# A group's products by the probabilities' high half first, and eight pieces from scores to products

## The chip, the cores and the metric

One core of a Trainium2 chip runs the whole program. The metric is the device time of one execution in microseconds (us). Five engines work beside each other, each through its own list of instructions in order: TensorE (PE, matrix products into PSUM; PEld are its weight loads), VectorE (DVE), ScalarE (ACT), GpSimd (POOL) and SyncE (SP), which here issues most of the DMA transfers.

## The reference

Three layers follow each other on float32 data, 4 sequences of 576 rows, 8 heads of 64:

```python
scores = scale * np.matmul(q, k.transpose(0, 1, 3, 2))      # 4 x 8 x 576 x 576
scores = np.where(block_i >= block_j, scores, -1e9)         # blocks of 64 rows
attn = exp(scores - max) / (sum + 1e-09)
x = np.matmul(attn, v)                                      # then to 2304 x 512
xn = x / rms * rms_g
y = (silu(xn @ w_gate) * (xn @ w_val)) @ w_out              # 512 -> 1536 -> 512
expert_idx = np.argmax(softmax of normed y @ normed experts)
out = gate_w * (relu(y @ w1[e]) @ w2[e])                    # 8 experts, 512 -> 1024 -> 512
```

## The kernel before, in words

Every float32 operand is split into two float16 halves, a high one and the low remainder, and a product is made of three: high by high, high by low, low by high.

**Attention.** Each sequence is cut into tiles of 128 query rows (the fifth has 64), and a tile into groups of heads: 8 heads in one group for the first tile of a sequence, groups of 4 for the second, of 2 for the others; 60 groups in all. A group goes through these steps. `att_qk` (L308) makes the scores on TensorE. `att_max` (L344, VectorE) and `att_exp` (L361, ScalarE) make the probabilities pf. `att_split` (L386) makes the high half ph on ScalarE (L414) and the low half pl on GpSimd (L417; for a sequence's last tile on VectorE, L412) and has SyncE's queue transpose each by DMA into pth and ptl (L423), of which there are two buffers each. `att_pv` (L433) multiplies them with the values: per head and block of 128 keys three products, all adding up in one PSUM tile av: pth with the values' high half, pth with their low half, ptl with their high half (L450 to L452). After a tile's last group `fin_all` (L514) normalizes the result over VectorE, ScalarE and GpSimd and transposes it by DMA into xT (L512), the input of the gate layer. The tile hl that xT is transposed from has one buffer. The first 11 groups are transposed on TensorE instead (L395).

**Gate layer.** Rows are taken in 9 units of 256. For each unit and each of six column steps, `gate_mm` (L519) makes g and v, `gate_t`, `gate_a`, `gate_b` turn them into hT, and `out_mm` (L560) adds hT by w_out into two accumulators o, one for each 128 rows; there are two buffers of o in PSUM. `out_ev` (L572) empties them at a unit's end: a copy, the low half, and a square in place (L579) that is the last to read o. The copy for the second 128 rows also waits for the one buffer R, which a DMA transpose into x2T (L583) has to have read.

**Order.** The groups up to the third unit are put in place by a scheduler that orders each engine's list by simulated times. From there on TensorE's list is written out by hand (L1018 to L1054): the gate layer of six units is a row of 216 pieces, two of out_mm and four of gate_mm for each column step, 12 products of 256 columns or 6 of 512 each. The scores of a group go in at every 4.8 pieces (EVERY) and its products LATER = 7 pieces after its scores:

```python
a = min(pieces - 1, int((g - first) * EVERY) + 2)
due.setdefault(a, []).append(("qk", g))
due.setdefault(min(pieces, a + LATER), []).insert(0, ("pv", g))
```

The other engines' lists are still ordered by the scheduler. **Experts.** After the last unit the tokens are sorted by expert, gathered, and multiplied with the experts' weights (from about 620 us on); that order is written by hand for all engines.

Of the kernel before, what the change touches and what calls it, by code (L numbers as in the profile page):

```python
# [18 lines left out]
P = 128  # L19
# [12 lines left out]
def attention_moe_moe(ctx: ExitStack, tc: tile.TileContext, q, k, v, w_gate, w_val, w_out, rms_g, emb, tau, w1, w2, out):  # L32
    nc = tc.nc
    B, H, S, D = q.shape
# [50 lines left out]
    st_p = p1.enter_context(tc.tile_pool(name="st", bufs=3))  # L85

    FS, PET = 5, 4
    AHEAD, NW0, NW1, NW2, WLAG, NLAG, LOADS, PREPS, PRI, EVERY, LATER = 3, 4, 2, 2, 2, 1, 3, 1, 300, 4.8, 7


    idn = const.tile([P, P], F32, name="idn")
# [131 lines left out]
    nat, qT, kT, vT = {}, {}, {}, {}  # L223

    def rows_of(t):
        return min(P, S - t * P)
# [203 lines left out]
    NOSYNC = mybir.DependencyInfo(mybir.DependencyClass.NoSync, mybir.DependencyReason.DATA)  # L430
    gv = {}

    def att_pv(b, t, heads):  # L433
        pth, ptl = pt_t.pop((b, t, heads[0]))
        if (b, t) not in av:
            av[b, t] = [ps_a.tile([P, H, D], F32, tag="av", name="av"), None]
        a = av[b, t]
        n = rows_of(t)
        nkb = t + 1
        last = t == NTT - 1  # L440
        for j, h in enumerate(heads):
            o = a[0][0:n, h, :]
            for kb in range(nkb):
                kn = min(P, S - kb * P)
                if last:
                    lh, ll = pth[0:kn, kb, 64 * j:64 * j + 64], ptl[0:kn, kb, 64 * j:64 * j + 64]
                else:
                    lh, ll = pth[:, j * nkb + kb, :], ptl[:, j * nkb + kb, :]
                vv = vT[b, kb]
                for i, (x, w) in enumerate(((lh, vv[0:kn, h, 0:D]), (lh, vv[0:kn, h, D:2 * D]), (ll, vv[0:kn, h, 0:D]))):  # L450
                    first = a[1] is None
                    mm = nc.tensor.matmul(out=o, lhsT=x, rhs=w, start=first, stop=(h == H - 1 and kb == nkb - 1 and i == 2), skip_group_check=True)  # L452
                    if first:
                        a[1] = mm.ins
                    else:
                        tc.add_manual_dep(mm.ins, a[1].name, NOSYNC, reason="the first of a bank starts it")
        if heads[-1] == H - 1:
            fin_all(b, t)

# [54 lines left out]
    def fin_all(b, t):  # L514
        for z in (fin_a, fin_b, fin_c, fin_d1, fin_d2, fin_d3):
            z(b, t)
# [358 lines left out]
    for u in range(NU):  # L875
        b, t = max((i, bt) for i, bt in enumerate(TILES) if spot[bt][0] == u)[1]
# [67 lines left out]
    def attend():  # L944
        attend_a()
        att_pv(*groups[state["g"] - 1])
# [71 lines left out]
    first = state["g"]  # L1018
    pieces = NFP * 6 * (NU - 3)
    due = {}  # L1020
    for g in range(first, len(groups)):
        a = min(pieces - 1, int((g - first) * EVERY) + 2)
# [23 lines left out]
    with tc.manual_schedule(engines={ENG.PE}):  # L1046
        for i in range(pieces + 1):
            for kind, g in due.get(i, []):
                if kind == "qk":
                    attend_a(LOADS + 1, PREPS + 1)  # L1050
                else:
                    att_pv(*groups[g])
            if i < pieces:
                piece(2 + i // (6 * NFP), i // 6 % NFP, i % 6)  # L1054
# [149 lines left out]
```

## Time and profile before

| | |
|---|---|
| median of 3 runs | 874.27 us (872.91 to 879.01) |
| the profiled execution | 875.68 us, its span 873.8 us |
| TensorE busy | 791.7 us, 91% |
| VectorE, ScalarE, GpSimd busy | 457.0, 449.6, 354.2 us |
| mean granted TensorE clock | 0.967 |

A timeline row gives the start in us from the span's start, the duration in us, the engine, the line of the kernel, the operation, its output and inputs, shapes and how many like it are merged (x12); in brackets how long the engine had been idle before it and whose end it waited for. SPq is SyncE's queue: the time of its rows is the issue of a transfer, not its flight. The granted clock is 1.00 at 2.4 GHz and 0.50 at 1.2 GHz.

### The profile page before, as it was taken

The page shows a single profiled execution, that of the slowest core. Times are in us where ns is not written, and L with a number is a line of the kernel's source. Part 1 is how long each engine was busy: PE and PEld are TensorE (multiplying, and loading weights), DVE is VectorE, ACT ScalarE, POOL GpSimd, SP SyncE. Part 2 cuts the span into 40 slices and gives each one's busy share as a digit, 9 for nine tenths or more (in the row PEclk, how much of TensorE's full clock was granted, in tenths as well). Part 3 has the DMA queues.
Part 4 walks back from the last instruction along what each step waited for, and adds up shares of the span by engine and source line. Part 5 has one row for each costly group of instructions (what it writes and reads, how often), then busy time and mean ns, then how long its engine had stood idle before and what let it go on. Part 6 is the DMA issues. An engine that isn't in the chain of part 4 may idle for free. (4 is left out here: it accounts for less than half of the span.)

```text
span 873.8 us, 21877 instructions
## 1 busy us (share of the span) xinstructions
PE 791.7 (91%) x8566; PEld 599.1 (69%) x8566; DVE 457.0 (52%) x971; ACT 449.6 (51%) x929; POOL 354.2 (41%) x360
## 2 busy tenths in 40 slices
PE   2769799889899899899899999998989998999994
PEld 2669577668677677677677777757567776667771
DVE  6899978634356445356445453225451265462352
ACT  6988776856556655556555441223311364452352
POOL 5555466756444737434737322212322121302110
PEclk9889889989999999999999999999999999999998
DMA  8574799885777775767875341214546399797694
GB/s 240 158 193 140 180 235 225 151 161 104 134 154 137 122 145 104 148 134 132 136 135 100 65 92 23 49 43 105 169 123 210 83 281 315 187 334 199 158 261 131
DMA packets 297629, 135.37 MB, mean 155 GB/s; under 512 B 250844, under 2 KB 281735, under 8 KB 297514
## 3 DMA queue, kind: packets, MB, share of 16 engines
q1 hardware_dynamic: 289706, 117.26, 61.7%
q0 software_dynamic: 4016, 10.56, 4.0%
q10 hardware_dynamic: 3792, 6.03, 2.1%
q8 instruction: 70, 1.15, 0.6%
q14 instruction: 45, 0.37, 0.1%
HBM read 129.30 MB, written 10.25 MB: 160 GB/s over the span
## 5 line engine op out<-in xcount | busy, mean ns | idle before, releaser
L529 PE MATMUL g<-xT,wg 128*128 128x256 f16 x1296 | 159.2, 278 | 4.2 <-DVE t L546 3.1
L529 PE MATMUL v<-xT,wv 128*128 128x256 f16 x1296 | 156.2, 274 | 0.0
L566 PE MATMUL o<-wo,hT 128*128 128x512 f16 x648 | 153.0, 385 | 3.4 <-ACT o L579 3.1
L529 PEld LDWEIGHTS <-wg 128*128 128x128 f16 x1296 | 126.8, 100 | 28.4 <-issue 4.6
L529 PEld LDWEIGHTS <-wv 128*128 128x128 f16 x1296 | 123.7, 98 | 15.2
L753 PE MATMUL h<-xt,whi 128*128 128x128 f16 x1280 | 109.8, 219 | 1.7 <-DMA xt<-xg 1.7
L753 PE MATMUL h<-xt,wlo 128*128 128x128 f16 x640 | 108.5, 219 | 0.2 <-DVE wlo L720 0.2
L566 PEld LDWEIGHTS <-hT 128*128 128x128 f16 x648 | 61.3, 98 | 68.2 <-issue 5.6
L720 DVE SCALAR_TENSOR_TENSOR wlo<-raw,whi 128x1024 f16<-128x1024 f32 x64 | 76.6, 1222 | 59.5 <-ACT whi L719 53.8
L753 PEld LDWEIGHTS <-whi 128*128 128x128 f16 x1280 | 98.9, 98 | 6.5 <-issue 2.6
L777 PE MATMUL o<-whi,hl 128*128 128x512 f16 x320 | 97.5, 387 | 5.2 <-ACT whi L719 2.8
L554 POOL TENSOR_TENSOR hT<-h,hT 128x512 f16<-128x512 f32 x54 | 64.2, 1189 | 77.3 <-ACT hT L553 75.3
L719 ACT ACTIVATE whi<-raw 128x1024 f16<-128x1024 f32 x64 | 65.9, 1053 | 52.5 <-DMA raw<-in_moe_w_dram 39.5
L417 POOL TENSOR_TENSOR pl<-pf,ph 128x512 f16<-128x512 f32 x66 | 69.5, 1074 | 50.4 <-issue 43.4
L777 PEld LDWEIGHTS <-hl 128*128 128x128 f16 x480 | 46.8, 99 | 62.6 <-issue 12.8
L785 POOL DMA_INDIRECT out_dram<-ob,ido x18 | 20.1, 1116 | 158.9 <-ACTq L726 76.4
L353 DVE TENSOR_REDUCE nb<-sc 128x1 f32<-128x384 f32 (+3 forms) x88 | 54.0, 635 | 45.7 <-PE sc L321 45.5
L452 PE MATMUL av<-vT,ptl 128*128 128x64 f16 (+2 forms) x480 | 56.7, 197 | 23.2 <-DMA ptl<-pl 15.9
L452 PE MATMUL av<-vT,pth 128*128 128x64 f16 (+2 forms) x960 | 64.8, 197 | 10.3 <-DMA pth<-ph 7.4
L452 PEld LDWEIGHTS <-pth 128*128 128x128 f16 (+2 forms) x960 | 52.9, 104 | 20.8 <-DMA pth<-ph 9.3
L372 ACT ACTIVATE pf<-sc,nb 128x128 f32<-128x128 f32 (+3 forms) x128 | 65.9, 526 | 2.3 <-PE v L529 0.4
L452 PEld LDWEIGHTS <-ptl 128*128 128x128 f16 (+2 forms) x480 | 45.3, 104 | 28.1 <-DMA ptl<-pl 18.3
(215 smaller groups left out, 1284.7 us busy)
## 6 DMA issues: line engine op xcount, KB each, us to landing
raw<-in_moe_w_dram SPq DMA_DIRECT2D x172, 512.0 KB
st<-in_moe_w_out_dram SPq DMA_DIRECT2D x12, 512.0 KB
st<-in_moe_w_gate_dram SPq DMA_DIRECT2D x11, 512.0 KB
st<-in_moe_w_val_dram SPq DMA_DIRECT2D x11, 512.0 KB
x2s<-R ACTq DMA_DIRECT2D x18, 256.0 KB
nat<-in_k_dram SPq DMA_DIRECT2D x16, 256.0 KB
nat<-in_q_dram SPq DMA_DIRECT2D x16, 256.0 KB
nat<-in_v_dram SPq DMA_DIRECT2D x16, 256.0 KB
```

Source lines behind the costliest of these rows:

```text
L353: nc.vector.tensor_reduce(out=nb[:, z], in_=sc[:, 0:hpb * keys].rearrange("p (j k) -> p j k", k=keys), axis=AX.X, op=ALU.max)
L372: nc.scalar.activation(out=pf[:, j * keys:(j + 1) * keys], in_=scs[j // hpb][:, (j % hpb) * keys:(j % hpb + 1) * keys], func=ACTF.Exp, sca ...
L417: nc.gpsimd.tensor_tensor(out=pl[:, z:y], in0=pf[:, z:y], in1=ph[:, z:y], op=ALU.subtract)
L452: mm = nc.tensor.matmul(out=o, lhsT=x, rhs=w, start=first, stop=(h == H - 1 and kb == nkb - 1 and i == 2), skip_group_check=True)
L529: mm = nc.tensor.matmul(out=o[:, j, :], lhsT=w[cw][:, kt, f * P:(f + 1) * P], rhs=x[:, cx * KD + kt, :], start=(n == 0), stop=(n == 3 * KD ...
L554: nc.gpsimd.tensor_tensor(out=hT[1][fp], in0=h, in1=hT[0][fp], op=ALU.subtract)
L566: mm = nc.tensor.matmul(out=o, lhsT=hT[ch][f // 2][:, f % 2, j * P:(j + 1) * P], rhs=wo[cw][:, f, :], start=(f == 0 and n == 0), stop=(f = ...
L719: nc.scalar.activation(out=whi[l][c], in_=raw[l][c], func=ACTF.Copy, scale=ES)
L720: nc.vector.scalar_tensor_tensor(out=wlo[l][c], in0=raw[l][c], scalar=ES, in1=whi[l][c], op0=ALU.mult, op1=ALU.subtract)
L753: mm = nc.tensor.matmul(out=h[:, f, :], lhsT=w[:, kt, :], rhs=x[:, cx * KD + kt, :], start=(n == 0), stop=(n == 3 * KD - 1))
L777: nc.tensor.matmul(out=o, lhsT=x[:, cx, kt, :], rhs=w, start=(n == 0), stop=(n == 3 * K2 - 1))
L785: nc.gpsimd.indirect_dma_start(out=out, out_offset=bass.IndirectOffsetOnAxis(ap=(ido if ids is None else ids)[:, i:i + 1], axis=0), in_=ob ...
```

## The change

In `att_pv` the three products of a head and key block no longer stand together: a loop over the two halves is put around the heads, so that all products with pth of a group come first, two for each head and key block, and then all with ptl. LATER is 8 instead of 7.

```diff
--- before.py
+++ after.py
@@ -85,7 +85,7 @@
     st_p = p1.enter_context(tc.tile_pool(name="st", bufs=3))
 
     FS, PET = 5, 4
-    AHEAD, NW0, NW1, NW2, WLAG, NLAG, LOADS, PREPS, PRI, EVERY, LATER = 3, 4, 2, 2, 2, 1, 3, 1, 300, 4.8, 7
+    AHEAD, NW0, NW1, NW2, WLAG, NLAG, LOADS, PREPS, PRI, EVERY, LATER = 3, 4, 2, 2, 2, 1, 3, 1, 300, 4.8, 8
 
 
     idn = const.tile([P, P], F32, name="idn")
@@ -438,22 +438,22 @@
         n = rows_of(t)
         nkb = t + 1
         last = t == NTT - 1
-        for j, h in enumerate(heads):
-            o = a[0][0:n, h, :]
-            for kb in range(nkb):
-                kn = min(P, S - kb * P)
-                if last:
-                    lh, ll = pth[0:kn, kb, 64 * j:64 * j + 64], ptl[0:kn, kb, 64 * j:64 * j + 64]
-                else:
-                    lh, ll = pth[:, j * nkb + kb, :], ptl[:, j * nkb + kb, :]
-                vv = vT[b, kb]
-                for i, (x, w) in enumerate(((lh, vv[0:kn, h, 0:D]), (lh, vv[0:kn, h, D:2 * D]), (ll, vv[0:kn, h, 0:D]))):
-                    first = a[1] is None
-                    mm = nc.tensor.matmul(out=o, lhsT=x, rhs=w, start=first, stop=(h == H - 1 and kb == nkb - 1 and i == 2), skip_group_check=True)
-                    if first:
-                        a[1] = mm.ins
-                    else:
-                        tc.add_manual_dep(mm.ins, a[1].name, NOSYNC, reason="the first of a bank starts it")
+
+        for side in range(2):
+            for j, h in enumerate(heads):
+                o = a[0][0:n, h, :]
+                for kb in range(nkb):
+                    kn = min(P, S - kb * P)
+                    x = (pth, ptl)[side]
+                    x = x[0:kn, kb, 64 * j:64 * j + 64] if last else x[:, j * nkb + kb, :]
+                    vv = vT[b, kb]
+                    for w in (vv[0:kn, h, 0:D], vv[0:kn, h, D:2 * D])[:2 - side]:
+                        first = a[1] is None
+                        mm = nc.tensor.matmul(out=o, lhsT=x, rhs=w, start=first, stop=(side == 1 and h == H - 1 and kb == nkb - 1), skip_group_check=True)
+                        if first:
+                            a[1] = mm.ins
+                        else:
+                            tc.add_manual_dep(mm.ins, a[1].name, NOSYNC, reason="the first of a bank starts it")
         if heads[-1] == H - 1:
             fin_all(b, t)
 
```

TensorE's list at the first group whose stall stands among the rows below at 221.97 us, where its products begin (wv_192 and wo_193 are weight tiles, hT_3_204 the gate layer's result). Before:

```order
L529 MATMUL v<-xT,wv_192 128x256
L452 LDWEIGHTS pth
L452 MATMUL av<-vT,pth 128x64
L452 LDWEIGHTS pth
L452 MATMUL av<-vT,pth 128x64
L452 LDWEIGHTS ptl
L452 MATMUL av<-vT,ptl 128x64
```

And with the change:

```order
L566 MATMUL o<-wo_193,hT_3_204 128x512
L452 LDWEIGHTS pth
L452 MATMUL av<-vT,pth 128x64
L452 LDWEIGHTS pth
L452 MATMUL av<-vT,pth 128x64
L452 LDWEIGHTS pth
L452 MATMUL av<-vT,pth 128x64
```

The group now stands behind a piece of the output product that followed it before, and 16 products with pth stand ahead of the first of the 8 with ptl.

SyncE's queue where the second sequence ends and the third begins, the issues from 278 to 300 us (a shape is that of the transpose; nat are loads for a later tile). Before:

```order
L423 DMA_TRANSPOSE pth<-ph 128x8x128
L423 DMA_TRANSPOSE ptl<-pl 128x8x128
L512 DMA_TRANSPOSE xT<-hl 128x8x64
L423 DMA_TRANSPOSE pth<-ph 128x8x128
L423 DMA_TRANSPOSE ptl<-pl 128x8x128
L232 DMA nat<-in_k_dram 128x8x64
L232 DMA nat<-in_q_dram 128x8x64
L232 DMA nat<-in_v_dram 128x8x64
L423 DMA_TRANSPOSE pth<-ph 128x8x128
L423 DMA_TRANSPOSE ptl<-pl 128x8x128
L512 DMA_TRANSPOSE xT<-hl 128x8x128
```

And with the change:

```order
L423 DMA_TRANSPOSE pth<-ph 128x8x128
L423 DMA_TRANSPOSE ptl<-pl 128x8x128
L423 DMA_TRANSPOSE pth<-ph 128x8x128
L512 DMA_TRANSPOSE xT<-hl 128x8x64
L423 DMA_TRANSPOSE ptl<-pl 128x8x128
L232 DMA nat<-in_k_dram 128x8x64
L232 DMA nat<-in_q_dram 128x8x64
L232 DMA nat<-in_v_dram 128x8x64
L423 DMA_TRANSPOSE pth<-ph 128x8x128
L512 DMA_TRANSPOSE xT<-hl 128x8x128
L423 DMA_TRANSPOSE ptl<-pl 128x8x128
```

Both transposes of xT now stand between a group's pth and its ptl. The third sequence's end has the same two moves.

SyncE's queue ahead of a sequence's fourth and fifth tile, the issues from 233 to 243 us (pth of 128x5x128 belongs to the fifth tile). Before:

```order
L423 DMA_TRANSPOSE pth<-ph 128x8x128
L290 DMA_TRANSPOSE qT<-qd 128x8x128 x2
L423 DMA_TRANSPOSE ptl<-pl 128x8x128
L232 DMA nat<-in_k_dram 128x8x64
L232 DMA nat<-in_q_dram 128x8x64
L232 DMA nat<-in_v_dram 128x8x64
L423 DMA_TRANSPOSE pth<-ph 128x5x128
```

And with the change:

```order
L423 DMA_TRANSPOSE pth<-ph 128x8x128
L290 DMA_TRANSPOSE qT<-qd 128x8x128
L423 DMA_TRANSPOSE ptl<-pl 128x8x128
L232 DMA nat<-in_k_dram 128x8x64
L232 DMA nat<-in_q_dram 128x8x64
L232 DMA nat<-in_v_dram 128x8x64
L290 DMA_TRANSPOSE qT<-qd 128x8x128
L423 DMA_TRANSPOSE pth<-ph 128x5x128
```

One of the two transposes of qT has gone behind ptl and the loads. The same move stands once more, one sequence later.

## Rows read from the trace of the kernel before

**Rows 1.** the page, busy time of TensorE over the span (us, share, instructions)

```profile
PE 791.7 (91%) x8566; PEld 599.1 (69%) x8566; DVE 457.0 (52%) x971; ACT 449.6 (51%) x929; POOL 354.2 (41%) x360
```

**Rows 2.** stretches: us, busy of PE, PEld, DVE, ACT, POOL; granted clock, DMA share, GB/s

```profile
100.00:150.00 50.00, 44.58 (x458) 34.53 (x456) 41.11 (x81) 35.52 (x81) 29.10 (x27) 0.90 1.10 226
200.00:250.00 50.00, 46.73 (x546) 35.99 (x544) 22.56 (x61) 28.30 (x63) 30.39 (x29) 1.00 0.66 119
```

**Rows 3.** waits of TensorE, 150 to 560 us: total, times, longest (us)

```profile
PE av L452 <- DMA ptl<-pl: 15.9, 15, 2.2
PE av L452 <- DMA pth<-ph: 3.0, 2, 2.7
```

**Rows 4.** timeline of TensorE: start, us, instruction, idle before it and who ended it

```profile
173.73 0.20 PE L452 MATMUL av<-vT,ptl 128*128 128x64 f16 x1 [1.61 <-DMA ptl<-pl]
186.80 0.20 PE L452 MATMUL av<-vT,ptl 128*128 128x64 f16 x1 [0.74 <-DMA ptl<-pl]
221.97 0.20 PE L452 MATMUL av<-vT,ptl 128*128 128x64 f16 x1 [0.58 <-DMA ptl<-pl]
241.16 0.20 PE L452 MATMUL av<-vT,ptl 128*128 128x64 f16 x1 [2.21 <-DMA ptl<-pl]
294.36 0.20 PE L452 MATMUL av<-vT,ptl 128*128 128x64 f16 x1 [1.76 <-DMA ptl<-pl]
301.80 0.20 PE L452 MATMUL av<-vT,ptl 128*128 128x64 f16 x1 [0.61 <-DMA ptl<-pl]
369.52 0.20 PE L452 MATMUL av<-vT,ptl 128*128 128x64 f16 x1 [1.98 <-DMA ptl<-pl]
424.32 0.20 PE L452 MATMUL av<-vT,ptl 128*128 128x64 f16 x1 [1.73 <-DMA ptl<-pl]
432.17 0.20 PE L452 MATMUL av<-vT,ptl 128*128 128x64 f16 x1 [1.02 <-DMA ptl<-pl]
449.27 0.20 PE L452 MATMUL av<-vT,ptl 128*128 128x64 f16 x1 [0.95 <-DMA ptl<-pl]
473.28 0.20 PE L452 MATMUL av<-vT,ptl 128*128 128x64 f16 x1 [0.83 <-DMA ptl<-pl]
```

**Rows 5.** timeline of TensorE: two pieces of the output product, then the next piece

```profile
222.62 2.75 PE L566 MATMUL o<-wo,hT 128*128 128x512 f16 x12
225.21 1.47 PE L529 MATMUL g<-xT,wg 128*128 128x256 f16 x12
```

**Rows 6.** timeline of the SyncE queue: start and issue time of transposes

```profile
233.51 1.23 SPq L423 DMA_TRANSPOSE pth<-ph  x1
234.84 2.67 SPq L290 DMA_TRANSPOSE qT<-qd  x2
298.52 1.23 SPq L423 DMA_TRANSPOSE ptl<-pl  x1
299.85 1.29 SPq L512 DMA_TRANSPOSE xT<-hl  x1
```

**Rows 7.** timeline of GpSimd at the same place

```profile
298.45 1.16 POOL L510 TENSOR_TENSOR hl<-x,hl 128x512 f16<-128x512 f32 x1
```

**Rows 8.** stretches after two longer waits, columns as in rows 2

```profile
190.00:195.00 5.00, 4.47 (x25) 2.69 (x25) 0.91 (x3) 0.48 (x2) 2.40 (x4) 0.50 1.00 220
369.50:375.00 5.50, 5.48 (x68) 4.42 (x70) 1.85 (x5) 2.30 (x4) 2.84 (x3) 0.69 1.03 191
```

**Rows 9.** timelines of TensorE and ScalarE: output product, and the square that frees its buffer

```profile
190.53 2.72 PE L566 MATMUL o<-wo,hT 128*128 128x512 f16 x6 [3.09 <-ACT o L579]
320.18 2.75 PE L566 MATMUL o<-wo,hT 128*128 128x512 f16 x12
321.06 0.19 ACT L579 ACTIVATION_READ_ACCUMULATOR o<-o 128x1 f32 x1
451.06 2.75 PE L566 MATMUL o<-wo,hT 128*128 128x512 f16 x12
451.76 0.19 ACT L579 ACTIVATION_READ_ACCUMULATOR o<-o 128x1 f32 x1
```

## The prediction

> **What bounds the kernel now.** I read the page first: TensorE is busy for 91% of the span [rows 1], so the end is set by its work and by the gaps in it. Then the stretches of 50 us. In the attention-and-gate part, from 200 us on, TensorE is busy 46.7 of 50 us at the full clock while VectorE, ScalarE and GpSimd do 22 to 31 [rows 2]: TensorE alone is the limit, and only its waits can be saved. In the stretch from 100 to 150 us it is different: VectorE is busy 41 of 50 us and the DMA engines are loaded above their count (share 1.10) [rows 2], so an order of TensorE's products is not what sets that part's length. Third, the list of waits: from 150 to 560 us TensorE sits idle 15.9 us for the transposed low half ptl, in 15 waits, and 3.0 us for the high half pth, in 2 [rows 3]. Each of the 15 sits at the same place in the timeline: a group's first two products, with pth, start, the third needs ptl, and since the products run in order, everything behind it stands too, the other 14 pth products and the gate products alike [rows 4].
>
> **The change, part by part.**
>
> *The number of instructions* does not change: the same products and weight loads, in another order. It costs nothing by itself.
>
> *High half first.* After a wait the other 22 products of a group of 24 and the next instruction follow within 222.62 - 221.97 = 0.65 us [rows 4, 5], 0.03 us each. Fourteen more pth products now stand ahead of the first ptl product: 14 x 0.03 = 0.41 us more time for ptl to land. It hides work of 0.41 us under the flight and no more; it cannot remove a wait of 2 us.
>
> *One piece more.* Two pieces of the output product take 225.21 - 222.62 = 2.59 us [rows 5], so a piece is 1.30 us of TensorE work, and each group's products now come that much later after its scores. Together ptl gets 1.71 us.
>
> *What that removes.* I count the waits of the manually ordered part. The first two of the 15, 1.61 and 0.74 us [rows 4], lie in the overlap of the scheduled part with it, and I leave them as they are. That leaves 15.9 - 2.35 = 13.55 us in 13 waits. Taken singly only 2.21, 1.76, 1.98 and 1.73 us [rows 4] exceed 1.71. But two things come on top. First, a group's lead contains the products of the group before it. Where that group's stall goes, the lead shrinks by it. This holds for the waits at 301.80 us (0.61, after 1.76) and 432.17 us (1.02, after 1.73) [rows 4]. Second, the queue order moves, as the order of the change shows. At those same two places, where a batch ends, the transpose of xT now stands between pth and ptl, and on GpSimd hl stands ahead of pl. In the trace xT came after ptl and its issue took 1.29 us [rows 6], hl took 1.16 us [rows 7]; I charge 1.2 us, since the two lie beside each other; the bounds are 0, if hl is long ready, and 2.45, if they add up. Residues: 0.61 + 1.76 - 1.71 + 1.2 = 1.86 us, and 1.02 + 1.73 - 1.71 + 1.2 = 2.24 us, with 0.05 and 0.02 us at 294.36 and 424.32 us. At 241.16 and 369.52 us, the longest waits, the order helps: ptl stood behind two transposes of qT, 2.67 us to issue [rows 6], and now stands behind one, so it gains 1.3 us beside the 1.71 and nothing is left. Sum: 13.55 - 4.17 = 9.4 us gained, between 6.9 and 11.8 by the bounds of the xT price.
>
> *The clock.* After the wait of 1.98 us the granted clock of the next 5.5 us was 0.69 [rows 8]: 5.5 x 0.31 = 1.7 us lost to products at the lower level, 1.2 GHz. No other of the 13 waits lies in a stretch that shows this (200 to 250 us holds 2.21 us and has 1.00 [rows 2]). With that wait gone I take 1.7 us; the bounds are 0 and 1.7.
>
> *What is late next.* The output accumulators. At a unit's start the second output piece overwrites a buffer that ScalarE's square must have left. At 320.18 us that piece starts 1.30 us later, at 321.48, and the square ended at 321.06 + 0.19 = 321.25; at 451.06 us it is 452.36 against 451.95 [rows 9]. The slack is 0.23 and 0.41 us. TensorE arrives there earlier by the stall taken out just ahead, 0.95 us at the second place [rows 4], so 0.95 - 0.41 = 0.5 us comes back there and, with a stall of about half a microsecond, 0.3 at the first: 0.8 us, between 0 and 1.2.
>
> *The xT of a finished tile* starts one piece, 1.30 us, later. The tile's unit begins 9 pieces or more after its last products, more than 11 us, and I charge nothing; if that cover were gone, each of the six units would lose up to 1.30 us.
>
> *The scheduled parts*, up to about 190 us, get the high-half-first order too and, through it, another order on every engine. What this is worth the trace does not show. TensorE's sum there is the same, VectorE and the DMA queues carry that part [rows 2], and I take 0. The bounds are 3.0 us either way, the size of the waits for pth there [rows 3]: they may vanish or come once more.
>
> Sum: 9.4 + 1.7 - 0.8 = 10.3 us. The profiled execution took 875.68 us, so 865.4; it lies 1.41 us above the median of the runs, and against that median, 874.27, the forecast is **864 us**.
>
> *A rule against it.* The third transposed group's pth was issued at 233.51 us [rows 6], while the group two before it, which held the same of two buffers, had finished its products when the output product began at 222.62 us [rows 5]: 10.9 us to spare, of which the change uses 1.30. The Trainium skill (Perfetto Trace Analysis, Identifying Performance Opportunities) reads a repeating gap on the saturated engine as a possible lack of buffers for the next tile. By that rule a greater distance would only hold the buffers longer, the transposes would start a piece later, and the result would be that of the first rival below. The trace does not agree with it here: the 10.9 us speak against it.
>
> **The rivals.**
>
> *The piece is given back* (chance 0.20). The pth and ptl of a later group start later by as much as the products moved, because the two buffers of each, or the queue in front of them, free later. Then only the 0.41 us of the first part remain: of the nine listed waits in that part 7.98 us are left, of the other four, 1.88 us in all, some 0.2; the gain is 13.55 - 8.2 = 5.3 us, no clock comes back, 0.8 goes to the accumulators: 4.5 us, **869.8 us**. For it speaks that SyncE's queue is in order and that xT, which itself waits for the moved products, now stands ahead of ptl at batch ends; against it the 10.9 us.
>
> *The scheduled part gains too* (0.19). The 1.61 and 0.74 us [rows 4] and the 3.0 us for pth [rows 3] go with the rest: 864 - 5.35 = **858.6 us**. For it: those are waits for the same tiles. Against it: they lie where DMA is full.
>
> *Slower: the accumulators become the bound* (0.07). At the first unit's start TensorE waited 3.09 us for the square [rows 9], and the next 5 us ran at clock 0.50 [rows 8], another 2.5 us. If the products that used to stand between the two output pieces now stand behind both, and the other five unit starts all wait like this, they cost 5 x 5.59 = 28 us against the 10.3 gained: 17.7 us slower, **892 us**. It decides from the point where the square ends later than the second output piece, a slack of 0.23 and 0.41 us at two of the starts [rows 9]; to be over 1% slower, four of five starts must lose the full price. Against it: the transpose x2T that holds the square up stands no later in the queue now.
>
> *No gain* (0.02): the scheduled part loses what the manual part gains, 874 us.
>
> **How the numbers follow.** The forecast has 0.52, with a range of its own of 860 to 868 (3.0 us of the scheduled part, and the bounds of the xT price). The bound of what a measurement can tell is 1%, or 865.5 us; some six tenths of the forecast's range lie below it. Faster by over 1%: 0.32 + 0.19 = 0.51. Within 1%: 0.20 + 0.20 + 0.02 = 0.42. Slower: 0.07. The range of 855 to 872 us takes in the forecast, the first two rivals and their spread, and leaves out the accumulators.
>
> **What would show it.** Right: the wait for ptl from 150 to 560 us falls from 15.9 to about 6 us, most of it at the two batch ends and in the overlap; no wait at the places of 241.16 and 369.52 us, and the clock there at 1.00; TensorE's busy time the same but for that clock; a wait for the square of under 1 us at the unit starts. Wrong: ptl waits of the same number, each shorter by about 0.4 us (the piece given back); waits for the output accumulators or for xT of a microsecond or more at most unit starts; or a first 190 us longer or shorter by more than 3 us, which would say that the scheduler's new order outweighs what was changed on purpose.

## The result, and the profile after

The change is slower: 882.62 us (876.4 to 886.45, 20 runs) against 877.37 us (871.74 to 883.28, 20 runs) of the kernel before; the ratio is 1.0059, 95% interval 1.0035 to 1.0082. That is 5.2 us more where 10.3 us less was forecast, outside the range of 855 to 872 us and inside the 1% that counted as no change. (3.1 us of the distance from 864 to 882.62 are the kernel before itself, 877.37 us in 20 runs for 874.27 in the three of the forecast.) The profiled execution has a span of 880.9 us and a mean clock of 0.962.

The page's busy line of the kernel after answers to [rows 1]; below it stands that of kernel 12, the kernel before profiled once more as a control. A stretch answers to [rows 2]:

```profile
PE 802.4 (91%) x8566; PEld 606.8 (69%) x8566; DVE 457.3 (52%) x971; ACT 448.5 (51%) x929; POOL 354.1 (40%) x360
```

```profile
PE 798.0 (91%) x8566; PEld 602.4 (69%) x8566; DVE 458.4 (52%) x971; ACT 449.7 (51%) x929; POOL 355.3 (41%) x360
```

```profile
200.00:250.00 50.00, 48.07 (x547) 37.63 (x545) 23.69 (x60) 27.43 (x59) 27.14 (x26) 0.97 0.62 117
```

In that stretch TensorE is busy 48.07 us for 46.73, at a granted clock of 0.97 for 1.00. The same 8566 instructions keep TensorE busy 10.7 us longer than in the profile of before. An edit that only takes waits out leaves the busy time as it is, so this is a hint that part of the loss is inside TensorE's work. It is no proof: in the control the kernel before is itself 6.3 us above its other profile. The waits of TensorE from 150 to 560 us, answering to [rows 3]:

```profile
PE av L452 <- DMA ptl<-pl: 11.0, 8, 1.9
PE av L452 <- DMA pth<-ph: 4.8, 4, 2.3
PE o L566 <- ACT o L579: 1.9, 3, 0.7
```

The waits for ptl are fewer (8 for 15), but two waits for pth have joined them, and the one wait for an accumulator, 3.09 us [rows 9], has become three of 1.9 us in all. TensorE's timeline, the waits of the hand-ordered part that answer to [rows 4] and [rows 9]:

```profile
196.39 0.59 PE L566 MATMUL o<-wo,hT 128*128 128x512 f16 x1 [0.46 <-ACT o L579]
229.13 0.26 PE L452 MATMUL av<-vT,ptl 128*128 128x64 f16 x3 [1.93 <-DMA ptl<-pl]
263.50 0.22 PE L452 MATMUL av<-vT,pth 128*64 128x64 f16 x1 [0.87 <-DMA pth<-ph]
309.22 0.26 PE L452 MATMUL av<-vT,ptl 128*128 128x64 f16 x3 [1.45 <-DMA ptl<-pl]
327.27 0.38 PE L566 MATMUL o<-wo,hT 128*128 128x512 f16 x1 [0.73 <-ACT o L579]
358.82 0.26 PE L452 MATMUL av<-vT,ptl 128*128 128x64 f16 x3 [1.56 <-DMA ptl<-pl]
391.83 0.25 PE L452 MATMUL av<-vT,pth 128*64 128x64 f16 x2 [1.20 <-DMA pth<-ph]
439.03 0.26 PE L452 MATMUL av<-vT,ptl 128*128 128x64 f16 x3 [1.36 <-DMA ptl<-pl]
457.03 0.38 PE L566 MATMUL o<-wo,hT 128*128 128x512 f16 x1 [0.69 <-ACT o L579]
```

From 200 us on that is 9.8 us (ptl 6.3, pth 2.1, accumulators 1.4) for 13.5 before. The waits at the former 241.16 and 369.52 us are gone, as forecast; those at 309.22 and 439.03 us are the two ends of a sequence; the other four, at 229.13, 263.50, 358.82 and 391.83 us, were not forecast. The first of these is not wholly new: the same group waited 0.58 us before [rows 4] and 1.58 us in the control.

One source of longer work is seen in the groups of a sequence's last tile. They have 30 products, as each of the two heads has four key blocks of 128 rows and a fifth of 64. TensorE's timeline of one of them before, then the same group after:

```profile
379.18 0.25 PE L452 MATMUL av<-vT,pth 128*64 128x64 f16 x2
...
379.55 0.20 PE L452 MATMUL av<-vT,ptl 128*64 128x64 f16 x1
379.68 0.25 PE L452 MATMUL av<-vT,pth 64*64 64x64 f16 x2
379.76 0.19 PE L452 MATMUL av<-vT,ptl 64*64 64x64 f16 x1
379.88 0.25 PE L452 MATMUL av<-vT,pth 128*64 128x64 f16 x2
...
380.59 0.28 PE L529 MATMUL g<-xT,wg 128*128 128x256 f16 x1
```

```profile
382.62 1.16 PE L452 MATMUL av<-vT,pth 128*64 128x64 f16 x20
383.71 0.84 PE L452 MATMUL av<-vT,ptl 128*64 128x64 f16 x10
384.48 0.72 PE L529 MATMUL v<-xT,wv 128*128 128x256 f16 x5
```

Read the starts, not the durations. Inside a shape products follow each other by 0.03 us; the first of a 64-row block starts 0.13 us behind its neighbour (379.55 to 379.68), and so does the first of 128 rows behind it (379.76 to 379.88). Each step between the two shapes costs about 0.1 us. Before, a group takes such a step four times, in and out of the fifth block of each head, and lasts 380.59 - 379.18 = 1.41 us. With the halves apart every head meets its fifth block twice: eight steps and 384.48 - 382.62 = 1.86 us. (1.86 - 1.41) / 4 = 0.11 us a step; I take 0.115 from the mean of the groups. There are 16 such groups: 16 x 0.46 = 7.4 us, an estimate that takes the four groups of the scheduled part, where other instructions stand between the products, to cost the same.

Last, where in the program the time is lost. ScalarE's square of the first unit's second rows and of the last but one unit, before and after, and the first of the two in kernel 17, whose lists up to there are those of before:

```profile
189.79 0.58 ACT L579 ACTIVATE o<-o 128x512 f32<-128x512 f32 x1 [0.24 <-DVE R L578]
...
587.50 0.58 ACT L579 ACTIVATE o<-o 128x512 f32<-128x512 f32 x1 [0.76 <-DVE R L578]
```

```profile
195.65 0.58 ACT L579 ACTIVATE o<-o 128x512 f32<-128x512 f32 x1 [0.76 <-DVE R L578]
...
593.22 0.58 ACT L579 ACTIVATE o<-o 128x512 f32<-128x512 f32 x1 [0.76 <-DVE R L578]
```

```profile
196.18 0.58 ACT L579 ACTIVATE o<-o 128x512 f32<-128x512 f32 x1 [0.24 <-DVE R L578]
```

In this pair 5.9 us are gone by the end of the scheduled part, and the hand-ordered part takes 397.6 us after for 397.7 before (399.6 in the control). But kernel 17 comes to that square later still, with the lists of before. A pair of profiles therefore does not place the loss; kernels 5 and 9 below, each of one part alone, do.

### The profile page after: what moved, and what is told of

It reads as the page before. It is cut to its first block, busy times and chain, and to the rows that moved or that the text cites. A ratio compares the mean times of both kernels' runs of the same rounds, so it can differ in the third digit from the quotient of the medians.

```text
span 880.9 us, 21875 instructions
## 1 busy us (share of the span) xinstructions
PE 802.4 (91%) x8566; PEld 606.8 (69%) x8566; DVE 457.3 (52%) x971; ACT 448.5 (51%) x929; POOL 354.1 (40%) x360
## 4 chain that ended last, share of the span: by engine, by line
PE 20%; DMA 19%; issue 11%; ACT 2%; POOL 2%; DVE 2%; POOLq 0%; SPq 0%; ACTq 0%; DVEq 0%
DMA out_dram<-ob,ido 13%; PE o L566 7%; PE g L529 5%; PE v L529 4%; DMA x2T<-R 1%; DMA out_dram<-ob,to 1%; PE av L452 1%; DMA tbl<-pay,pi 1%; PE h L753 1%; DMA raw<-in_moe_w_dram 1%; POOL pl L417 0%; DMA xT<-hl 0%; DMA pth<-ph 0%; DMA ptl<-pl 0%; PE sc L318 0%
## 5 line engine op out<-in xcount | busy, mean ns | idle before, releaser
L529 PE MATMUL g<-xT,wg 128*128 128x256 f16 x1296 | 156.5, 276 | 3.2 <-DVE t L546 2.7
L353 DVE TENSOR_REDUCE nb<-sc 128x1 f32<-128x384 f32 (+3 forms) x88 | 54.4, 636 | 38.3 <-PE sc L321 38.1
L753 PEld LDWEIGHTS <-wlo 128*128 128x128 f16 x640 | 62.6, 98 | 2.1 <-issue 1.2
L777 PE MATMUL o<-wlo,hl 128*128 128x512 f16 x160 | 62.4, 390 | 1.2 <-DVE wlo L720 1.1
L546 DVE SCALAR_TENSOR_TENSOR t<-t,g 128x512 f32<-128x512 f32 x54 | 36.7, 679 | 41.2 <-ACT t L540 41.0
L764 DVE SCALAR_TENSOR_TENSOR hl<-h,hl 128x1024 f16<-128x1024 f32 x20 | 24.4, 1221 | 64.0 <-ACTq L726 48.0
```

The costliest lines, as they stand in the source:

```text
L353: nc.vector.tensor_reduce(out=nb[:, z], in_=sc[:, 0:hpb * keys].rearrange("p (j k) -> p j k", k=keys), axis=AX.X, op=ALU.max)
L529: mm = nc.tensor.matmul(out=o[:, j, :], lhsT=w[cw][:, kt, f * P:(f + 1) * P], rhs=x[:, cx * KD + kt, :], start=(n == 0), stop=(n == 3 * KD ...
L546: nc.vector.scalar_tensor_tensor(out=t, in0=t, scalar=1.0, in1=g, op0=ALU.add, op1=ALU.mult)
L753: mm = nc.tensor.matmul(out=h[:, f, :], lhsT=w[:, kt, :], rhs=x[:, cx * KD + kt, :], start=(n == 0), stop=(n == 3 * KD - 1))
L764: nc.vector.scalar_tensor_tensor(out=hl[:, 1], in0=h, scalar=0.0, in1=hl[:, 0], op0=ALU.max, op1=ALU.subtract)
L777: nc.tensor.matmul(out=o, lhsT=x[:, cx, kt, :], rhs=w, start=(n == 0), stop=(n == 3 * K2 - 1))
```

## The experiments

In all of them the loop of `att_pv` runs over one list `seq` of (half of the probabilities, head, key block, half of the values), taken from two orders: `full` is that of before, `hi1` that of the change. `last` marks a sequence's last tile, `man` the groups of the hand-ordered part. Ratios are to the kernel before on the same chip, with 95% intervals.

**Is it the steps?** Kernel 1 only moves the 64-row block behind the others; 2 puts high half first in the last tile alone; 3 and 4 are the change with other orders of the last tile.

```diff
 1 (LATER 7)  +seq = sorted(full, key=lambda x: last and x[3] == nkb - 1)
 2 (LATER 7)  +seq = hi1 if last else full
 3 (LATER 8)  +seq = full if last else hi1
 4 (LATER 8)  +seq = sorted(hi1, key=lambda x: last and x[3] == nkb - 1)
```

Expected of 1: 

> The kernel before, with LATER 7; only in a sequence's last tile the products with the fifth key block, which has 64 rows, are put behind all products with the four blocks of 128 rows. Every engine's list has the same rows in the same order as before; only which block a product of that tile takes is moved. In the trace of before a group of the last tile takes 1.40 us for 30 products, a group of the fourth tile 0.70 us for 24, and the products of 64 rows start 0.13 us behind the one in front, where others follow by 0.03. Theory A (each step between 128 and 64 contracted rows costs about 0.115 us, which is (1.86 - 1.40)/4 from the change's groups with eight steps for four): with two steps a group takes 1.17 us, 16 groups give 3.7 us, 0.996 of the time before. Rival B (what costs is the step from one head to the other in that tile, 0.23 us each, one before and three with the change): here there are three, a group takes 1.86 us, 7.4 us slower, 1.008. Rival C (the time was lost to the scheduler's other order, the last tile's groups have nothing to do with the end): 1.40 to 1.86 us or not, no change, 1.000.

Measured: 1.002 (0.9995 to 1.0046). TensorE's timeline of the run, the end of a last-tile group that starts at 261.75 us:

```profile
262.50 0.20 PE L452 MATMUL av<-vT,ptl 128*64 128x64 f16 x1
262.62 0.24 PE L452 MATMUL av<-vT,pth 64*64 64x64 f16 x2
262.71 0.19 PE L452 MATMUL av<-vT,ptl 64*64 64x64 f16 x1
262.74 0.22 PE L452 MATMUL av<-vT,pth 64*64 64x64 f16 x2
262.80 0.19 PE L452 MATMUL av<-vT,ptl 64*64 64x64 f16 x1
262.93 0.60 PE L566 MATMUL o<-wo,hT 128*128 128x512 f16 x2
```

The group lasts 262.93 - 261.75 = 1.18 us, where theory A said 1.17. The step from head to head inside the 64-row block (262.71 to 262.74) costs nothing, which ends rival B. But the end does not come earlier: the size of a step is right, its worth at the end here is not.

Expected of 2: 

> The kernel before, with LATER 7; only the groups of a sequence's last tile have all products with the high half first, as in the change. Theory A: eight steps between 128 and 64 rows in place of four, 1.86 us a group, 16 x 0.46 = 7.4 us slower, 1.008 (5.5 us and 1.006 if the four groups in the scheduled part hide theirs). Rival B: the same, three steps between heads for one. Rival C: no change, 1.000.

Measured: 1.0117 (1.0083 to 1.0151), with groups of 1.86 us. That is 10.3 us, at least the price of the steps, which ends rival C as it stood.

Expected of 3: 

> The change (high half first, LATER 8), but the groups of a sequence's last tile keep the order of before, three products to a key block. Theories A and B: those groups take 1.40 us again, 7.4 us under the change's 882.6: 875.2 us, 0.997 to 0.998 of before. Rival C: stays at the change's time, 1.006, with the first unit's squares 5 to 6 us later than before.

Measured: 0.9978 (0.9953 to 1.0002). 0.81% or 7.1 us under the change (some 3 us either way), for 7.4 computed. This kernel also has another order from the scheduler behind the first such group, so the 7.1 us are not the steps alone.

Expected of 4: 

> The change, but in a sequence's last tile the products with the fifth key block of 64 rows come behind all others, those with the high half ahead of those with the low half. Theory A: two steps between 128 and 64 rows for eight, 1.17 us a group, 16 x 0.69 = 11.0 us under the change: 871.6 us, 0.993 of before. Rival B: seven steps between heads, 1.40 + 6 x 0.23 = 2.8 us a group, 15 us over the change: 897 us, 1.023. Rival C: the change's time, 1.006.

Measured: 1.0029 (1.0005 to 1.0053), a miss, though its groups last 1.18 us. This kernel, too, differs from the change in what the scheduler made of everything behind the first such group (waits from 198 to 560 us: 18.8 us, for 10.9 in kernel 3). So the next four leave the scheduled part alone.

**The hand-ordered part alone.** Here every engine's list is as before up to that part.

```diff
 5 (LATER 8)  +seq = hi1 if man else full
 6 (LATER 8)  +seq = hi1 if man and not last else full
 7 (LATER 8)  +seq = sorted(hi1 if man and not last else full, key=lambda x: man and last and x[3] == nkb - 1)
 8 (LATER 8)  +seq = full
```

Expected of 5: 

> The change confined to the part whose TensorE order is written by hand: high half first in its groups, LATER 8; the groups of the scheduled part keep the order of before, and every engine's list is as before up to there. Theory A (steps between 128 and 64 rows, 0.115 us each, cost 0.46 us in each of the 12 last-tile groups of this part, 5.5 us, against some 4 to 6 us of waits removed): 0.999 to 1.002 of before. Theory C (the scheduled part's other order cost most of it: the first unit's square came 5.9 us later in the change's trace than in that of before, of which four groups x 0.46 are steps): the same here, 0.999 to 1.001, since the scheduled part is as before. If the scheduled part's order is not at fault, 1.004 to 1.006, close to the change.

Measured: 0.9974 (0.9948 to 1.0).

Expected of 6: 

> As the run before, but the last tile's groups keep the order of before, so no step is added anywhere. Theory A: 5.5 us (0.6%) faster than the run before it; 0.993 to 0.996 of before, with last-tile groups of 1.40 us and the waits for ptl from 200 to 560 us at 5 to 8 us for 13.5. Rival (what is saved at a wait comes back at the next, since a group's time ahead of its transposes is made of the products in front): 0.999 to 1.000.

Measured: 0.9952 (0.9919 to 0.9985).

Expected of 7: 

> As the run before, and in the last tile's 12 groups of the hand-ordered part the products of the 64-row block come behind the others (two steps in place of four). Theory A alone: groups of 1.18 us, 12 x 0.22 = 2.7 us (0.3%) faster than the run before it, 0.990 to 0.993 of before. Rival (a group shortened by 0.22 us gives as much less time to the transposes behind it, and the next waits grow): no faster than the run before it.

Measured: 0.9912 (0.9872 to 0.9953).

Expected of 8: 

> LATER 8 alone, the products in the order of before. If the piece more is what takes the waits away (13.5 us in 13 waits, the most of them under 1.3 us; the lead from a group's scores to its products grows by 1.3 us), 7 to 9 us faster, 0.990 to 0.992. If the piece is given back, because scores, maxima and halves of a group come later too (in the change's trace the time from the high half's end to the products was 7.8 us at the third transposed group as before), 2 to 4 us, 0.996 to 0.998.

Measured: 0.9937 (0.9906 to 0.9969).

The order 5, 6, 7 is that of their steps (eight, four, two to a group), though each difference alone lies within the intervals. From 5 to 6 it is 1.9 us where the steps taken out come to 5.5, from 5 to 7 5.5 us where they come to 12 x 0.68 = 8.2: what the steps cost at the end is less sure than what they add to a group. Confined to this part the change is not slower than before, so the scheduled part carries the loss. And LATER 8 alone does as well as with high half first: 8 against 6.

**The scheduled part alone**, all with LATER 7, and the kernel before once more as a control:

```diff
 9   +seq = full if man else hi1
 10  +seq = hi1 if g < need[1] else full           # the 11 groups transposed on TensorE
 11  +seq = hi1 if not man and g >= need[1] and not last else full
 14  +seq = hi1 if last and b == 0 else full       # the last tile of the first sequence
```

Expected of 9: 

> The complement of the run with the change confined to the hand-ordered part: high half first in the groups of the scheduled part alone (last tile of the first sequence included), LATER 7, the order of before in the hand-ordered part. If the two parts add up, 1.0059 - (0.9974 - 1) = 1.0085 of before, 7 us slower, with the first unit's first square at 181 to 185 us instead of 175 to 177. If the scheduled part's loss is taken back later (the hand-ordered part starts with groups further ahead), 1.000 to 1.004.

Measured: 1.0052 (1.0016 to 1.0087).

Expected of 10: 

> High half first only in the first 11 groups, whose probabilities are transposed on TensorE; LATER 7, all other groups in the order of before. In the change's trace TensorE stood 3.27 us at 36.48 us for ptl of such a group, whose two subtractions on VectorE came at 35.74 us, where before they came at 32.84 and 34.04 us; the gate layer began at 59.46 us for 56.73. If that is where the scheduled part loses, 2 to 4 us slower, 1.002 to 1.005, and the gate layer begins 2 to 3 us later. If the loss is in the later groups, 1.000.

Measured: 0.9999 (0.9969 to 1.0029).

Expected of 11: 

> High half first only in the scheduled part's groups that are transposed by DMA, without the last tile's; LATER 7. The first 56 us are as before. If the loss of the scheduled part lies with these groups, 1.003 to 1.006; if with the groups transposed on TensorE and with the steps of the last tile, 1.000.

Measured: 0.999 (0.9959 to 1.0021).

Expected of the control, 12: 

> The kernel before, unchanged, for the spread of its own stages: 1.000 of before, between 0.997 and 1.003; the first unit's first square between 175 and 180 us (five profiles with the same order of the scheduled part gave 175.4 to 179.6), the last unit's last square to the end 238 to 243 us.

Measured: 0.9977 (0.9935 to 1.0019); the last but one unit's square at 589.23 us for 587.50, so single profiles of one kernel differ by 2 us there.

Expected of 14: 

> High half first only in the four groups of the first sequence's last tile, which lie in the scheduled part; LATER 7. Theory A: 16 more steps between 128 and 64 rows, 1.8 us, 1.002. If the scheduler's other order behind them is what costs in the scheduled part (1.0052 with all its groups, 1.000 and 0.999 with the others alone), 1.004 to 1.006.

Measured: 1.0057 (1.0022 to 1.0092), as much as all groups of the scheduled part together. The neighbours cost nothing, although in the change's trace a group transposed on TensorE shows TensorE's longest new wait:

```profile
36.48 0.39 PE L452 MATMUL av<-vT,ptl 128*128 128x64 f16 x4 [3.27 <-DVE ptl L398]
```

That wait is not the edit's: at the same place it is 3.23 us in kernel 17 and 3.04 us in kernel 13, which have the order of before there, and 1.34 us in both profiles of before. Of the 5.0 us of kernel 14 (interval 1.9 to 8.1), four groups of steps are 1.8 us; the other 3.2 may come from the scheduler's other order behind those groups. Its trace does not show where: between 56 and 200 us TensorE waits 6.4 us for ptl, for 2.5 in the control, but 15.5 us in all for 15.6, and the first unit's second square comes at 189.96 us, as early as before. Kernel 2 has the steps of these four groups and of the twelve in the hand-ordered part: 1.0117 against 1.0057 is 5.3 us (some 4 either way) for the 12 x 0.46 = 5.5 of the twelve.

**Why the piece more gives so little.** Theory T: a finished tile's normalization waits for the tile's last products and stands, on VectorE, ahead of the next group's maximum; its transpose xT stands in SyncE's queue ahead of the next pth. With the products a piece later both come a piece later. VectorE ahead of the group of 221.16 us before, of the same group after, and of the same group in the control (L498 is the normalization, L353 the maximum, one for each of the group's two heads):

```profile
209.29 0.74 DVE L498 SCALAR_TENSOR_TENSOR x<-x,fin,g_b 128x512 f32<-128x512 f32 x1
209.96 1.28 DVE L353 TENSOR_REDUCE nb<-sc 128x1 f32<-128x512 f32 x2
```

```profile
214.08 0.69 DVE L353 TENSOR_REDUCE nb<-sc 128x1 f32<-128x512 f32 x1 [0.15 <-PE sc L321]
215.28 0.75 DVE L498 SCALAR_TENSOR_TENSOR x<-x,fin,g_b 128x512 f32<-128x512 f32 x1 [0.51 <-POOL fin L493]
215.95 0.68 DVE L353 TENSOR_REDUCE nb<-sc 128x1 f32<-128x512 f32 x1
```

```profile
211.00 0.75 DVE L498 SCALAR_TENSOR_TENSOR x<-x,fin,g_b 128x512 f32<-128x512 f32 x1 [0.78 <-POOL fin L493]
211.67 1.28 DVE L353 TENSOR_REDUCE nb<-sc 128x1 f32<-128x512 f32 x2
```

The group's scores began at 209.14, 213.41 and 209.11 us. After them the first maximum came 0.82 us later before, 0.67 us in the change and 2.56 us in the control; in the change the second stands behind the normalization and came 2.54 us after the scores. So maxima behind a normalization, and as late, occur with the order of before too, and these rows do not show that the change made them late: the half of the theory on VectorE stays open. Between the change and the control the wait differs behind the issue: ptl was issued 10.2 us behind the scores in both (8.9 us before), and TensorE's wait for it ended 5.5 us behind the issue in the change, 4.2 us in the control; why, these rows do not tell. The half on SyncE's queue has more for it. SyncE's queue at the second group of a last tile, before and after:

```profile
250.66 1.84 SPq L512 DMA_TRANSPOSE xT<-hl  x1
252.60 1.24 SPq L423 DMA_TRANSPOSE pth<-ph  x1
```

```profile
258.06 1.29 SPq L512 DMA_TRANSPOSE xT<-hl  x1
259.44 1.23 SPq L423 DMA_TRANSPOSE pth<-ph  x1
```

Its products were due at 256.71 us before, 4.1 us behind the issue of pth; now at 262.63 (263.50 less the wait of 0.87), 3.2 us behind it. At these two groups TensorE waits for pth, 0.87 to 1.49 us, in all eight profiles with LATER 8 for every group, and in none with LATER 7.

```diff
 13  LATER 8, products in the order of before
-        due.setdefault(min(pieces, a + LATER), []).insert(0, ("pv", g))
+        due.setdefault(min(pieces, a + LATER - (groups[g][2][-1] == H - 1)), []).insert(0, ("pv", g))
 15 (LATER 8)  +seq = sorted(full, key=lambda x: man and last and x[3] == nkb - 1)
 16            kernel 7 with LATER 9
 17 (LATER 7)  +seq = sorted(full, key=lambda x: man and last and x[3] == nkb - 1)
```

Expected of 13: 

> As the run with LATER 8 alone (0.9937 of before), but the group that ends a tile comes 7 pieces after its scores, as before; all others 8. Theory T: part of the piece is given back because a finished tile's normalization on VectorE and its transpose xT in SyncE's queue, which wait for the tile's last products, stand ahead of the next group's maximum and of its pth; with the last products a piece later these come a piece later too. Then the waits at the second group of a fourth tile (1.73 us at 224 us in the run with LATER 8) fall under 0.3, the two waits for pth in the last tiles (2.7 us) are gone, and the waits at tile-ending groups are as before (2.21, 0.61, 1.98, 1.02): 6 to 7 us of waits from 200 to 560 us for 11.1, so 0.988 to 0.991. If T is wrong, the waits at the second groups and for pth stay, and the time is that of LATER 8 or 2 us more, 0.994 to 0.996.

Measured: 0.9962 (0.993 to 0.9994). The waits of TensorE from 198 to 560 us in kernel 8 (those for ptl and pth), in 13, and in 16:

```profile
PE av L452 <- DMA ptl<-pl: 7.3, 8, 1.8
PE av L452 <- DMA pth<-ph: 2.7, 2, 1.5
```

```profile
PE av L452 <- DMA ptl<-pl: 10.0, 8, 2.0
```

```profile
PE o L566 <- ACT o L579: 8.1, 5, 3.1
PE av L452 <- DMA ptl<-pl: 1.8, 6, 0.4
```

In 13 the two waits for pth are gone, the fourth tiles' second groups (225.87 and 355.20 us) wait for nothing, and the waits stand at the groups that end a tile. So the tile's last products decide where the waits stand, as theory T has it. What this is worth did not come: 10.0 us of waits where 6 to 7 were expected, and no faster than 8.

Expected of 15: 

> LATER 8, the products in the order of before but with the 64-row block's behind the others in the last tile's groups of the hand-ordered part. Theory A: 12 x 0.22 = 2.7 us under LATER 8 alone, 0.990 to 0.991; then high half first gives nothing more than 0.001 to the run that has both (0.9912). If the shorter groups come back as waits, 0.993 to 0.994.

Measured: 0.9913 (0.988 to 0.9946), 874.13 us for 881.28. With 7 it is the fastest, and the simpler of the two.

Expected of 16: 

> The fastest run so far (high half first in the hand-ordered part, last tile in three products to a block with the 64-row block last; 0.9912 of before) with LATER 9. If a piece more takes 1.3 us off each of the seven ptl waits left there (8.7 us), 0.984 to 0.987. If it is given back at the tile ends, as theory T has it, 0.990 to 0.993; the waits for pth behind xT then grow by up to 1.3 us each.

Measured: 0.9934 (0.9901 to 0.9966). A further piece does take the waits for ptl out, and the accumulators take their place: TensorE waits up to 3.1 us for the square at two unit starts. This was the prediction's slower rival, one piece further on than it stood.

Expected of 17: 

> The kernel before, LATER 7; the products of the 64-row block come behind the others in the last tile's 12 groups of the hand-ordered part alone; all lists are otherwise the same, row by row. Theory A: 12 x 0.22 = 2.7 us faster, 0.997. If the shorter groups come back as waits for ptl, since a group's time ahead of its transposes is made of the products in front, 1.000 to 1.002, as in the first run, where the 16 groups of all four sequences were so ordered (1.002 where 0.996 was expected).

Measured: 0.9998 (0.9969 to 1.0026).

Expected of the repeat of 1: 

> The first run again, with the 64-row block last in all 16 groups. If its 1.002 was the spread of the measurement, 0.996 to 0.998; if the four groups of the scheduled part lose what the twelve gain, 1.000 to 1.003 here and 0.997 in the run beside it.

Measured: 0.9986 (0.9956 to 1.0016). In 17 the waits for ptl from 198 to 560 us are 15.5 us, in the repeat 13.8, for 12.9 and 13.5 in the two profiles of before. At LATER 7 a shorter group may give part of what it saves back as waits; whether and how much, these intervals do not tell.

## Why the prediction was wrong

*The number of instructions does not change, it costs nothing.* This step failed. The instructions are the same, but not their neighbours: 0.115 us for each step between 128 and 64 contracted rows, 64 steps more. The Trainium skill (TensorEngine Tiling (Array Packing), Key Properties) says that changing the tiling mode drains TensorE. The trace has 0.13 us to the next start for 0.03 where the contracted rows change; that this is such a change of mode, no run here shows. The price could have been read before: a group of 30 products lasted 1.41 us and one of 24 only 0.70, and I had priced a product from the 24 alone [rows 4, 5]. Cost: 7.4 us by the groups' lengths, 7.1 us between the change and kernel 3, with the scheduler's order in it. The steps alone did not turn the sign: with them the hand-ordered part was still 2.3 us faster (kernel 5).

*The scheduled parts: 0, between -3.0 and 3.0.* This step failed too, and it is what turns the gain into a loss: 4.6 us slower in kernel 9 (0.0052 x 882.5), above the bound of 3.0, though the interval, 1.4 to 7.7, reaches below it. Kernel 14 puts all of it on the first sequence's last tile. 1.8 us of it are the steps above; for the rest the cause stays open.

*High half first: 0.41 us.* Right in kind, with waits for ptl of 6.7 us in 5 for 7.3 in 8, and too small to see in the time: 0.9952 with it against 0.9937 without (kernels 6 and 8), 0.9912 against 0.9913 (7 and 15).

*One piece more, and what it removes: 9.4 us.* The mechanism was right, the size was not: this term is mis-sized. LATER 8 alone gives 5.6 us (0.0063 x 883.15, interval 2.7 to 8.3). At the two ends of a sequence the residues were 1.45 and 1.36 us for 1.86 and 2.24, and the two longest waits left nothing. But waits of 1.93, 1.56, 0.87 and 1.20 us, 5.6 in all, stand where a tile has ended; those for pth are new, the first had 0.58 us before and 1.58 in the control.

*The xT of a finished tile: 0.* This step mis-sized the one above in part. I looked at who reads xT, the gate unit 11 us later, and not at who is queued behind it. I had written that xT stands between a group's pth and ptl at a sequence's end and stopped there; it stands ahead of a pth after every fourth tile too, and there the two waits for pth are, 2.1 us in the change. How much more it cost is not shown, as kernel 13, which takes these waits away, was no faster.

*The first rival, the piece given back*, was therefore partly right, through SyncE's queue, as it had named, and not through the buffers: the 10.9 us to spare on those [rows 5, 6] were there.

*The accumulators: 0.8 us lost.* Right in kind and nearly in size: two waits from 200 us on, 1.4 us.

*The clock: 1.7 us gained.* Wrong: the places forecast had no low stretch, but others had. Stretches of the kernel after, and of the control, with the granted clock as the third number from the end:

```profile
228.90:234.40 5.50, 5.27 (x40) 3.34 (x41) 1.37 (x4) 0.63 (x1) 1.77 (x2) 0.69 0.33 70
391.60:397.10 5.50, 5.26 (x47) 4.01 (x48) 1.25 (x3) 0.28 (x1) 0.85 (x1) 0.69 0.99 112
```

```profile
242.50:248.00 5.50, 5.33 (x58) 4.00 (x60) 1.66 (x5) 2.30 (x4) 2.83 (x3) 0.69 1.04 198
374.60:380.00 5.40, 5.18 (x76) 4.07 (x77) 3.18 (x7) 3.23 (x6) 2.70 (x3) 1.00 1.20 205
```

The kernel after has the low stretch behind its waits of 1.93 and 1.20 us. The control, the same kernel as before, has it behind 2.02 us at 242.67 and not behind 2.49 us at 374.82, the other way round than [rows 8]. In two executions of the kernel before, one of two waits of 2.0 to 2.5 us had it behind it and the other not; I took one execution's draw for a property of the place.

The account, an estimate from single profiles and medians: 7.4 us of steps, 3.2 for the scheduled part beyond its steps, 4.8 of waits left (9.8 against 4.17 + 0.8), 1.7 of clock: 17.1 us for the 15.5 by which forecast and result differ, which the interval of 2 us either way and the spread of kernel 14 (3 us) allow. By runs alone, the two parts of the change, kernels 5 and 9 (which leaves LATER at 7), come to 4.6 - 2.3 = 2.3 us with 4 either way, for the 5.2 measured. Two of the marks named beforehand came, a first 190 us longer by more than 3 and a busy time that grew. As marks they were weak: kernel 17 has the first with the lists of before, the control most of the second.

## What to carry to other kernels

Before moving products, write down their shapes in order, old and new, and count the places where the contracted rows change; a group whose mean start distance is larger than its neighbours' (47 ns for 29 here) is the sign. When an operation is put later, price what waits for its result on engines and queues that work in order, and then everything queued behind that, not only the reader of the result. Profile the kernel before at least twice, and read off a pair of profiles only what is larger than the difference of those two. Where a scheduler orders the rest, test an edit in the part that it cannot reorder first: there the same edit went from 0.6% slower to not slower, and LATER 8 with the 64-row block last and otherwise the order of before was 0.9% faster.

## What the runs showed of the hardware

A product whose contracted rows differ from those of the one in front (64 after 128, or back) starts 0.12 to 0.13 us behind it, otherwise 0.03 (0.05 for the second behind a step); head and output column may change without cost, as in the 0.03 us from 262.71 to 262.74 us. In the kernel before the granted clock over the next 5.5 us was 0.69 after waits of 1.98 and 2.02 us, and 1.00 after waits of 2.21 and 2.49 us, at places that changed between two executions. The expert part, the same instructions in every kernel here, took 238.3 to 243.6 us from the last square to the end in 20 profiles: a single profile cannot settle a difference of that size. The first unit's second square came at 189.6 to 196.2 us in kernels whose lists up to there are those of before.
